# Three float32r passes over exactly split operands in place of seven- and twenty-product float32 schemes, in a scan and SwiGLU kernel

## The chip, the core and the metric

The kernel runs on one core of one Trainium2 chip. The metric is the device time of one execution in microseconds. The kernel before takes 394.63 us (median of 3 runs, 394.61 to 395.21).

## What is computed

A selective-state scan (Mamba-2) over 4 sequences, 8 heads, 768 positions, 32 channels a head and 16 states, followed by a feed-forward network over the resulting 3072 tokens of 256 channels. All arrays of the scan are float32; the three weight matrices come in as float64 in memory. Cut to what matters:

```python
for c in range(nc):                                   # chunks of 32 positions
    cum = np.cumsum(log_a[:, :, sl], axis=-1)
    L = np.exp(cum[:, :, :, None] - cum[:, :, None, :]) * causal
    y[:, :, sl] = einsum(CB * L, xc) + einsum(Cc, state) * np.exp(cum)[..., None]
    state = decay_full * state + sum_j(Bc * xc * decay_from_j)
x = y.transpose(0, 2, 1, 3).reshape(3072, 256)
xn = x / np.sqrt(np.mean(x * x, -1, keepdims=True) + 1e-06) * rms_g
g = xn @ w_gate                                       # 256 x 1536
out = (g / (1 + np.exp(-g)) * (xn @ w_val)) @ w_out   # 1536 x 256
```

## The kernel before

**Tiling.** The 3072 tokens are 6 blocks of 512. A block is two pairs of scan chunks of 128 tokens (12 pairs in all). The channels of a token lie on the partitions, so `xn` is two tiles of 128 x 512; the 1536 features are 12 tiles of 128, taken as 6 pairs `j` of feature tiles.

**Weights.** They are fetched as 18 pieces of 4 KB a partition (`fetch`, line 164/167, into 6 rotating places), and decoded from float64 words to float32: the power of two on ScalarE (`power`, three steps at line 197), the mantissa on VectorE (`mantissa`, lines 216 and 219), their product on VectorE (`weight`, line 225).

**Scan.** For each pair, decays are spread by DMA from memory (`spread`), subtracted, exponentiated and masked (`ex`), B and C are transposed on TensorE (`turn`, line 529), products formed (`products_of_block`, line 579) and multiplied by the decays (line 612), states carried on (`states`, lines 658 and 668), and the outputs formed (`outputs`, lines 644 and 716). `squares`, `norm_sums`, `norm_roots` and `norm_apply` (line 827) make `xn`. This is done for block b + 1 while block b's network runs.

**Gate and value products.** Blocks 1 to 5, and half of block 0's feature tiles, use a scheme of seven products for a 2 x 2 split (`product_gv`, line 931; its operands' sums are made by `combine_w` and `combine_x`). Each product k for a pair j is two matmuls (gate and value) of 128 x 128 weights by 256 columns. Partial sums are copied out by ScalarE (`taken_gv`, line 937) and added by VectorE (`total_gv`, line 943); then activation (line 197) and the hidden product (`hide_gv`, line 956, on VectorE or GpSimd). The rest of block 0 uses whole matmuls of 512 columns (`products_gv`, line 845) or, for the first two tiles, products of the values before normalization (line 855).

**Down products.** Block 0: 48 whole matmuls of 256 columns (`project`, line 963). Blocks 1 to 5: a scheme of twenty products for a 4 x 3 by 3 x 2 split (`product_o`, line 1052), each four matmuls of 128 columns; sums of hidden tiles (`sum_h`, line 1026) and of weights (line 1008) feed it, and `total_o` adds the products up in 26 steps (lines 1079 and 1083).

**Order.** A list of steps written out by hand gives the order in which every engine's instructions are issued; `idle` steps and `*2` marks put matmuls on constants into gaps. All matmuls are float32, but for bfloat16 matmuls on masks and constants (`idle`, line 317, and the fillers at line 88 among them). One matmul instruction in float32 appears in the trace as two weight loads and two matmul records.

Of the kernel before, what the change touches and what calls it, by code (L numbers as in the profile page):

```python
# [9 lines left out]
FP32 = mybir.dt.float32  # L10
I32 = mybir.dt.int32
# [5 lines left out]
AX = mybir.AxisListType  # L17


@with_exitstack  # L20
def kernel(
# [12 lines left out]

# [17 lines left out]
    NAR = BH * NC // 2  # L72

    const = ctx.enter_context(tc.tile_pool(name="const", bufs=1))
    raw = ctx.enter_context(tc.tile_pool(name="raw", bufs=3))
    ssd = ctx.enter_context(tc.tile_pool(name="ssd", bufs=2))
    cvt = ctx.enter_context(tc.tile_pool(name="cvt", bufs=2))
    nrm = ctx.enter_context(tc.tile_pool(name="nrm", bufs=2))
    ffn = ctx.enter_context(tc.tile_pool(name="ffn", bufs=2))
# [3 lines left out]

    fillers = []

    def filled(t, flat):
        for k in range(fillers.pop() if fillers else 0):
            nc.tensor.matmul(out=flat, lhsT=warm[:, 0:P], rhs=warm[:, 0:flat.shape[1]], start=True,
                             stop=True)
        return t  # L90

    def bank(name, shape):
        t = mm.tile(list(shape), FP32, tag="one", bufs=2, name=name)
        letters = "abc"[0:len(shape) - 1]
        flat = t.rearrange("p %s -> p (%s)" % (" ".join(letters), " ".join(letters)))
        return filled(t, flat[:, 0:min(256, flat.shape[1])])

    def pair_of_banks(name, slot):
        t = (mm if slot == 2 else pairs[slot].pool).tile([P, 2, 512], FP32, tag="pair%d" % slot,
                                                         name=name)  # L100
        return filled(t, t[:, 0, 0:256])


    pairs, later, sides = {}, {}, ("left", "right")
    for slot in (1, 0):
        pairs[slot] = ctx.enter_context(ExitStack())
        pairs[slot].pool = pairs[slot].enter_context(
            tc.tile_pool(name="first%d" % slot, bufs=1, side=sides[slot],
                         space=bass.MemoryType.PSUM))
# [4 lines left out]
    def load(p, queues=(nc.sync, nc.sync)):  # L114
        br = raw.tile([P, 2, NH, N], FP32, tag="br", name="br")
        cr = raw.tile([P, 2, NH, N], FP32, tag="cr", name="cr")
        st.setdefault(p, {}).update(B=br, C=cr)
        for i, queue in enumerate(queues):
            load_chunk(p, i, queue)
# [7 lines left out]
    def load_x(p, queue=nc.sync):  # L127
        b, c0 = divmod(2 * p, NC)
        st.setdefault(p, {})["x"] = raw.tile([P, 2, NH, D], FP32, tag="xr", name="xr")
        for i in range(2):  # L130
            sl = slice((c0 + i) * P, (c0 + i + 1) * P)
            queue.dma_start(out=st[p]["x"][:, i], in_=x[b, :, sl, :].rearrange("h s n -> s h n"))


    wgv = const.tile([P, 2, 2, DF], FP32, name="wgv")
    wg, wv = wgv[:, 0], wgv[:, 1]
    wo = const.tile([P, NF, DM], FP32, name="wo")
# [15 lines left out]
    def fetch(*ks):  # L153
        for k in ks:
# [7 lines left out]
            r = raw.tile([P, shape[0], 2 * shape[1]], I32, tag="wr", name="wr", bufs=6)  # L162
# [9 lines left out]

# [20 lines left out]
    def power(k):  # L199
        words16, (lo, hi), dst, shape = fetched[k]  # L200
        n = shape[1] * shape[2]
        e = cvt.tile([P, n], FP32, tag="e", name="e", bufs=4)
# [5 lines left out]
                             alpha=2.0 ** -20)  # L208
        activation(out=b16, in_=g, func=AF.Prelu, scale=-2.0 ** 27, bias=kinks[:, 2:3],
                             alpha=2.0 ** -20)  # L210
        parts[k, "e"] = b16.bitcast(BF16)

    def mantissa(k):
        words16, (lo, hi), dst, shape = fetched[k]
        m = cvt.tile(shape, I32, tag="m", name="m")
# [5 lines left out]

    def weight(k):
        words16, (lo, hi), dst, shape = fetched[k]
        e, f = parts.pop((k, "e")), parts.pop((k, "f"))
        nc.vector.scalar_tensor_tensor(out=dst, in0=f, scalar=2.0 ** -20, in1=e,  # L225
                                       op0=ALU.mult, op1=ALU.mult)

    a_sb = ffn.tile([NAR, 2 * P], FP32, tag="ob", name="a_sb", bufs=1)
# [3 lines left out]
    ones = const.tile([P, P], FP32, name="ones")  # L232
    upto = const.tile([P, P], FP32, name="upto")
    never = const.tile([P, P], FP32, name="never")
    after = const.tile([P, P], FP32, name="after")
    chunk_ones = const.tile([P, 2, P], FP32, name="chunk_ones")
# [7 lines left out]
    ident16 = const.tile([P, P], BF16, name="ident16")  # L244
    whole16 = const.tile([P, P], BF16, name="whole16")
# [4 lines left out]
    la = const.tile([P, NC, BH], FP32, name="la")  # L250
    laf = la.rearrange("p c h -> p (c h)")
    NG = 2 * NC * NB + 4
    early = nrm.tile([P, NC * BH + 2 * NG * NH], FP32, tag="xn", name="early", bufs=1)
    la0 = early[:, 0:NC * BH].rearrange("p (c h) -> p c h", c=NC)
    full, fsel = [early[:, NC * BH + k * NG * NH:][:, 0:NG * NH].rearrange(
        "p (g h) -> p g h", h=NH) for k in range(2)]
    la4 = [const.tile([P, 4, 4, NH], FP32, name="la4%d" % k) for k in range(2)]
    mids = const.tile([P, 2, P], FP32, name="mids")
    mid = mids[:, 0]
    first_four = slice(0, 4), slice(0, NH)  # L260

    def loaded_a():
        nc.sync.dma_start(out=a_sb, in_=a.rearrange("b h (q k) -> (b h q) k", k=2 * P))
# [50 lines left out]
    def idle(n):  # L314
        ps["idle"] = ps.get("idle") or bank("idle", (P, 256))
        for k in range(n):
            nc.tensor.matmul(out=ps["idle"], lhsT=warm[:, 0:P], rhs=warm, start=True, stop=True)

    def turn_a():
        ps["aT"] = aT = bank("aT", (P, 2, NAR))  # L320
        for k in range(2):
            nc.tensor.transpose(out=aT[:, k], in_=a_sb[:, k * P:(k + 1) * P],
                                identity=ident[0:NAR, 0:NAR])

    def clipped():
        nc.vector.tensor_scalar(
            out=la0.rearrange("p (q k) r -> p k r q", k=2),
            in0=ps.pop("aT").rearrange("p k (r q) -> p k r q", q=NC // 2), scalar1=1e-6,
            scalar2=1.0, op0=ALU.max, op1=ALU.min)

    def logs_again(g, n):
# [3 lines left out]
            in_=la0[:, c:c + n, b * NH:(b + 1) * NH].unsqueeze(2).to_broadcast([P, n, 4, NH]),  # L335
            func=AF.Ln)

    def minus_mid():
# [26 lines left out]
        "log": lambda: activation(out=la, in_=la0, func=AF.Ln), "mids": minus_mid,  # L365
# [7 lines left out]
    rows, ps = {}, {}  # L373

    def sums_of_logs(k):
        ps["r", k] = r_ps = bank("r_ps", (P, 2, P))
# [4 lines left out]
    def three_parts(k):  # L381
        r_ps = ps.pop(("r", k))
        first = nrm.tile([P, 2, P], BF16, tag="first", name="first", bufs=1)
        nc.vector.tensor_copy(out=first, in_=r_ps)
        rest = nrm.tile([P, 2, P], FP32, tag="rest", name="rest", bufs=1)
        nc.vector.scalar_tensor_tensor(out=rest, in0=first, scalar=later_part, in1=r_ps,
                                       op0=ALU.mult, op1=ALU.add)
        second = nrm.tile([P, 2, P], BF16, tag="second", name="second", bufs=1)
# [4 lines left out]

# [4 lines left out]
    def other_sums():  # L398
        ps["d"] = d_ps = bank("d_ps", (P, 2, NC, BH))
# [8 lines left out]
    def other_decays():  # L408
        activation(out=d_sb, in_=ps.pop("d"), func=AF.Exp)

# [3 lines left out]
    def chunk_sums():  # L414
        ps["c"] = full_ps = bank("full_ps", (P, NG * NH))
# [8 lines left out]
    def chunk_decays():  # L424
        activation(out=full.rearrange("p g h -> p (g h)"), in_=ps.pop("c"), func=AF.Exp)
        nc.gpsimd.tensor_tensor(out=fsel, in0=full,
                                in1=hmask.unsqueeze(1).to_broadcast([P, NG, NH]), op=ALU.mult)

    def chunk_column():
        nc.vector.reduce_sum(out=fcol, in_=fsel, axis=AX.X)  # L430


    Ls = {}

    def pair_tile(g):
        p = g // 2
        if p not in Ls and p < 4:
            Ls[p] = ssd.tile([P, 2, NH, P if p < 2 else HC], FP32, tag="L", name="L", bufs=2)
        elif p not in Ls:
            Ls["of", p // 2] = L = ssd.tile([P, 4, NH, HC], FP32, tag="L", name="L", bufs=2)  # L440
            for k in range(2):
                Ls[p - p % 2 + k] = L[:, 2 * k:2 * k + 2]
        return Ls[p][:, g % 2]
# [7 lines left out]
    def sums(p, half, e):  # L451
# [6 lines left out]
        for k, h in enumerate(heads):  # L458
            for i, r in enumerate(rows_of):
                for u in parts:  # L460
                    nc.tensor.matmul(out=e[u, i, k * n:(k + 1) * n],
                                     lhsT=sel[r, h:h + 1].to_broadcast([32, n]),
# [10 lines left out]
    def decay(p, half, e):  # L473
        pair_tile(2 * p)
        L = Ls[p][:, :, 4 * half:4 * half + 4] if p < 2 else Ls[p]
# [9 lines left out]
    def spread(g):  # L485
        b, c = divmod(g, NC)
        o = (c * BH + b * NH) * HC
        for u, r in enumerate(halves):
            nc.sync.dma_start(out=pair_tile(g)[r].rearrange("p h m -> p (h m)"),
                              in_=rowv[u, o:o + NH * HC].partition_broadcast(HC))  # L490

    def subtract(g, engine=nc.vector):
        b, c = divmod(g, NC)
        L = pair_tile(g)
# [4 lines left out]
    def exponential(g):  # L499
        L = pair_tile(g)  # L500
        activation(out=L, in_=L, func=AF.Exp)
        causal(L)

    def decays(g):
        subtract(g)
        exponential(g)

    def scale(p):
# [3 lines left out]
        for name, src, d in (("Cd", "C", to_i), ("Bd", "B", from_j))[0 if p < 2 else 1:]:  # L512
            s[name] = ssd.tile([P, 2, NH, N], FP32, tag=name, name=name)
            nc.vector.tensor_tensor(
                out=s[name], in0=s[src],
                in1=d[:, c0:c0 + 2, hs].unsqueeze(3).to_broadcast([P, 2, NH, N]), op=ALU.mult)

    def transposed(p):
        s = st[p]
        if "T" not in s:  # L520
            s["T"] = ssd.tile([P, 2, 4, P], FP32, tag="T", name="T")
        return s["T"]

    def turn(p):
        s = st[p]
        ps["t", p] = tp = bank("tp", (P, 2, 2, P))
        for k, src in enumerate((s["B"], s["C"])):
            for i in range(2):
                nc.tensor.transpose(out=tp[:, k, i], in_=src[:, i].rearrange("p h n -> p (h n)"),
                                    identity=ident)  # L530

    def turned(p, copy):
        copy(out=transposed(p)[:, :, 0], in_=ps["t", p][:, 0])

    def turned_of(p, scaled, t):
        scaled(transposed(p)[:, :, 1 + t], ps["t", p][:, 1], tmask[:, t:t + 1])

    def turned_of_both(p):
        shape = [P, 2, 2, P]
        nc.vector.tensor_tensor(  # L540
            out=transposed(p)[:, :, 1:3], in0=ps["t", p][:, 1].unsqueeze(2).to_broadcast(shape),
# [917 lines left out]
```

## Time and profile before

| what | value |
|---|---|
| median of the runs | 394.63 us |
| the profiled execution: its span from first to last instruction | 395.6 us |
| matmul records | 3833 |
| VectorE, ScalarE, GpSimd busy | 287.7, 233.6, 160.8 us |
| TensorE clock granted, mean | 0.999 of full |
| memory read, written | 22.64, 3.74 MB |

The profiled execution has no time of its own beside its span; the span is 1.0 us above the median. Spans of instructions include the latency of the engine, so what an instruction occupies is read from the distance of starts. "PE" is TensorE's matmuls and "PEld" its weight loads, "DVE" VectorE, "ACT" ScalarE, "POOL" GpSimd, "SP" the queue that issues most DMAs. "L931" is line 931 of the kernel before.

### The profile page before, as it was taken

The numbers are of one execution on the slowest core, as the hardware profiler recorded it, in microseconds if no ns is written. First come the engines' busy times: TensorE is split into PE (matmuls) and PEld (weight loads), VectorE is DVE, ScalarE is ACT, GpSimd is POOL, SyncE is SP. The second block draws the span as 40 slices with busy tenths as digits, with TensorE's granted clock in tenths as the row PEclk, the third lists the DMA queues.
The fourth block names the chain that finished last, engine by engine and source line by source line (L and its number), as shares of the span: only waits on it lengthen the run. The fifth ranks groups of instructions, "written<-read, shape, count | busy, mean of one in ns | idle before, by whom it ended". The sixth has DMA issues, their size and how long they took to land.

```text
span 395.6 us, 9626 instructions
## 1 busy us (share of the span) xinstructions
PE 387.5 (98%) x3833; PEld 331.9 (84%) x3833; DVE 287.7 (73%) x588; ACT 233.6 (59%) x483; POOL 160.8 (41%) x178
## 2 busy tenths in 40 slices
PE   8998999999999999999999999999999999999996
PEld 5674488878888899888889888899888899988995
DVE  6998999988657968484897765676754487465574
ACT  3988987968689393446661543676345750455410
POOL 2243253774638467102573610465402064211271
PEclk9999999999999999999999999999999999999999
DMA  8889985486002428201414002001100000100001
GB/s 125 220 161 245 203 164 155 142 170 133 0 1 68 56 83 137 83 2 30 107 35 83 13 2 68 2 15 36 42 1 3 0 8 27 55 0 2 2 2 53
DMA packets 92533, 27.01 MB, mean 68 GB/s; under 512 B 77416, under 2 KB 86344, under 8 KB 92488
## 3 DMA queue, kind: packets, MB, share of 16 engines
q1 hardware_dynamic: 90408, 26.26, 29.7%
q8 instruction: 30, 0.49, 0.5%
q10 hardware_dynamic: 2080, 0.13, 0.4%
q14 instruction: 15, 0.12, 0.1%
HBM read 22.64 MB, written 3.74 MB: 67 GB/s over the span
## 4 chain that ended last, share of the span: by engine, by line
PE 77%; DVE 10%; ACT 3%; issue 3%; DMA 3%; SPq 3%; DVEq 0%; ACTq 0%
PE gate L931 26%; PE o L1052 21%; PE val L931 19%; PE o L963 3%; PE y L716 2%; SPq L125 2%; DVE m L219 2%; DMA sq<-roots 1%; DMA br<-in_B_dram 1%; PE g L579 1%; DVE m L216 1%; ACT L L197 1%; DVE wgv L225 1%; DVE S L668 1%; DVE c L943 1%
## 5 line engine op out<-in xcount | busy, mean ns | idle before, releaser
L943 DVE TENSOR_TENSOR c<-val,p 128x512 f32<-128x512 f32 x99 | 67.5, 687 | 40.2 <-PE val L931 27.7
L937 ACT COPY p<-gate 128x512 f32<-128x512 f32 x99 | 56.8, 582 | 60.7 <-PE gate L931 56.1
L956 POOL TENSOR_TENSOR hid<-c 128x256 f32<-128x256 f32 x40 | 32.9, 830 | 84.8 <-ACT c L197 82.5
L931 PE MATMUL gate<-tx,wgv 128*128 128x256 f32 x264 | 65.8, 383 | 0.0
L197 ACT ACTIVATE c<-c 128x256 f32<-128x256 f32 x99 | 39.3, 415 | 29.2 <-DVE c L943 28.8
L931 PEld LDWEIGHTS gate<-tx,wgv 128*128 128x128 f32 x264 | 48.9, 190 | 7.9 <-issue 0.7
L956 DVE TENSOR_TENSOR hid<-c 128x256 f32<-128x256 f32 x59 | 30.1, 519 | 17.8 <-ACT c L197 17.8
L1083 DVE TENSOR_TENSOR ob<-ob,o 128x128 f32<-128x128 f32 (+1 forms) x90 | 24.5, 299 | 20.9 <-PE o L1052 18.0
L482 POOL TENSOR_SCALAR_AFFINE_SELECT L<-L 64x512 f32<-64x512 f32 (+1 forms) x36 | 29.3, 813 | 19.9 <-ACT L L197 13.1
L1052 PE MATMUL o<-two,hid 128*128 128x128 f32 x280 | 36.3, 276 | 0.1
L1052 PEld LDWEIGHTS o<-two,hid 128*128 128x128 f32 x280 | 34.4, 192 | 1.1 <-issue 0.2
L931 PE MATMUL val<-tx,sw 128*128 128x256 f32 x132 | 33.9, 382 | 0.0
L931 PE MATMUL val<-xn,sw 128*128 128x256 f32 x132 | 33.7, 380 | 0.0
L931 PE MATMUL val<-xn,wgv 128*128 128x256 f32 x132 | 33.4, 381 | 0.2 <-DVE c L943 0.2
L931 PE MATMUL gate<-tx,sw 128*128 128x256 f32 x132 | 33.4, 382 | 0.0
L931 PE MATMUL gate<-xn,wgv 128*128 128x256 f32 x132 | 33.3, 381 | 0.0
L931 PEld LDWEIGHTS val<-xn,wgv 128*128 128x128 f32 x132 | 24.8, 190 | 4.0 <-PE gate L931 0.6
L931 PEld LDWEIGHTS val<-tx,sw 128*128 128x128 f32 x132 | 24.9, 190 | 3.8 <-DVE c L943 0.3
L931 PEld LDWEIGHTS gate<-xn,wgv 128*128 128x128 f32 x132 | 24.5, 190 | 3.8 <-DVE xn L827 0.4
L197 ACT ACTIVATE u<-gate 128x256 f32<-128x256 f32 (+1 forms) x37 | 14.8, 403 | 21.8 <-PE gate L931 19.4
L931 PEld LDWEIGHTS gate<-tx,sw 128*128 128x128 f32 x132 | 24.5, 190 | 3.4 <-issue 0.2
L931 PEld LDWEIGHTS val<-xn,sw 128*128 128x128 f32 x132 | 24.4, 190 | 3.3 <-issue 0.2
(196 smaller groups left out, 741.3 us busy)
## 6 DMA issues: line engine op xcount, KB each, us to landing
L<-rowd SPq DMA_DIRECT2D x32, 128.0 KB, 3.2
xr<-in_x_dram SPq DMA_DIRECT2D x24, 128.0 KB, 3.6
wr<-in_moe_w_out_dram SPq DMA_DIRECT2D x6, 512.0 KB, 3.8
out_dram<-ob SPq DMA_DIRECT2D x24, 128.0 KB, 2.0
wr<-in_moe_w_gate_dram SPq DMA_DIRECT2D x5, 512.0 KB, 4.0
wr<-in_moe_w_val_dram SPq DMA_DIRECT2D x5, 512.0 KB, 6.9
br<-in_B_dram SPq DMA_DIRECT2D x23, 64.0 KB, 3.5
cr<-in_C_dram SPq DMA_DIRECT2D x23, 64.0 KB, 2.7
```

Of the source, the lines that this page charges most:

```text
L125: queue.dma_start(out=st[p][name][:, i], in_=src[b, :, sl, :].rearrange("h s n -> s h n"))
L197: nc.scalar.activation(**operands)
L219: nc.vector.scalar_tensor_tensor(out=f, in0=lo.bitcast(U32), scalar=2.0 ** -32, in1=m, op0=ALU.mult, op1=ALU.add)
L482: nc.gpsimd.affine_select(out=L[r], in_=L[r], pattern=[[0, L.shape[1]], [1, HC]], compare_op=ALU.is_ge, fill=0.0, base=0, channel_multipli ...
L716: nc.tensor.matmul(out=y[2 * k + u][rows, (2 * n + i) * HC:(2 * n + i + 1) * HC], start=(k, u, rows.start) not in opened, stop=True, skip_ ...
L931: nc.tensor.matmul(out=dst[:, half[w]], lhsT=lhsT, rhs=rhs, start=(k in (1, 2, 5) and w == 0), stop=True, skip_group_check=True)
L937: nc.scalar.copy(out=t, in_=Xs[j])
L943: nc.vector.tensor_tensor(out=t, in0=Zs[j], in1=a, op=ALU.add)
L956: engine.tensor_tensor(out=hid[:, 2 * j + c // 10 - 1, c % 10 - 1], in0=u, in1=src[:, half[1]], op=ALU.mult)
L963: nc.tensor.matmul(out=o, lhsT=hid[:, f, k // 2, (k % 2) * P:(k % 2 + 1) * P], rhs=wo[:, f], start=opens, stop=(f == NF - 1), skip_group_c ...
L1052: nc.tensor.matmul(out=Os[blk, b][:, place * P:(place + 1) * P], lhsT=hidden_or_sum(u)[:, g], rhs=rhs, start=(blk, b) not in opened, stop= ...
L1083: nc.vector.tensor_tensor(out=o, in0=o, in1=src, op=ALU.add if what[0] == "+" else ALU.subtract)
```

## The change

1. **Gate and value products of blocks 1 to 5.** Every operand is split into a high part (float32r, the value times 1 - 2^-13, rounded on writing) and what is left. Three passes of float32r matmuls replace the seven-product scheme: high by high, scaled rest by rest (`X`, both into one bank), then ScalarE multiplies that bank in place by 1 + 2^-12 (`sc`), and a pass of mixed operands is added (`M`). All matmuls have 512 columns. The scheme's sums, the copies out of the banks and the additions go.
2. **Down products of blocks 1 to 5.** The same three passes, 256 columns each, over feature tiles 0 to 5 and 6 to 11 (`OX`, `os`, `OM`). The hidden tiles are split after the hidden product: high (ScalarE or VectorE), low (VectorE or GpSimd), mixed (VectorE). The twenty-product scheme with its sums and its 26 additions goes; an output bank is copied out once.
3. **Block 0** has ten of its twelve feature tiles as whole float32 matmuls of 512 columns; the first two and the down products stay in form.
4. **Weights** get a high, a low and a mixed part each, into the place of the raw words; each of the 18 pieces has a place of its own.
5. **Places.** All tiles on the chip come from shared rings of equal places (`Ring`, `Place`), with counted uses; the banks for products are three pairs and two single ones.
6. **Order.** The list of steps is new from the first to the last. Activation tables are loaded 32 times, before 26.

The diff, cut to its core (the new list of steps is left out, but for a stretch of it):

```diff
+class Ring:
+    def take(self, uses, what):
+        return Place(self, self.free.pop(0), uses, what)
...
-    wgv = const.tile([P, 2, 2, DF], FP32, name="wgv")
+    wgv = const.tile([P, 2, 2, DF], F32R, name="wgv")
...
-            r = raw.tile([P, shape[0], 2 * shape[1]], I32, tag="wr", name="wr", bufs=6)
+            whole = const.tile([P, 1024], I32, tag="wr%d" % k, bufs=1, name="wr")
...
+    def weight_high(k, scaled):
+        scaled(fetched[k][2], view(ws[k], fetched[k][3]), BELOW)
+    def weight_low(k, engine=nc.vector):
+        engine.tensor_tensor(out=low_parts[k], in0=view(ws[k], shape), in1=dst, op=ALU.subtract)
+    def weight_mixed(k):
+        first, scalar, second = (dst, -DOWN, low) if pieces[k][0] == "o" else (low, -UP, dst)
+        nc.vector.scalar_tensor_tensor(out=mixed, in0=first, scalar=scalar, in1=second,
+                                       op0=ALU.mult, op1=ALU.add)
...
-    def combine_w(j, k, engine=nc.vector):
-    def combine_x(blk, k, engine=nc.vector):
-    def product_gv(blk, k, j):
-    def taken_gv(blk, k, j):
-    def total_gv(blk, c, j):
-    def sum_h(blk, n, engine=nc.vector):
-    def total_o(blk, n):
...
+    def x_high(blk, t, scaled):
+        scaled(view(b, [P, TB], F32R), xns[blk][1][:, t], BELOW)
+    def x_mixed(blk, t):
+        nc.vector.scalar_tensor_tensor(out=view(b, [P, TB], F32R), in0=view(hb, [P, TB]),
+                                       scalar=-1.0 - DOWN, in1=xns[blk][1][:, t], op0=ALU.mult,
+                                       op1=ALU.add)
+    def x_scaled(blk, t):
+        nc.vector.scalar_tensor_tensor(out=view(b, [P, TB], F32R), in0=view(mb, [P, TB]),
+                                       scalar=UP, in1=view(hb, [P, TB]), op0=ALU.mult,
+                                       op1=ALU.add)
...
+    def gv_product(o, blk, f, m, t, x_part, w_part, start):
+        nc.tensor.matmul(out=o, lhsT=weights_of(m, t, f)[w_part], rhs=view(b, [P, TB], F32R),
+                         start=start, stop=True, skip_group_check=True)
+    def gv_whole(blk, f, m):
+        for t in range(2):
+            nc.tensor.matmul(out=o, lhsT=view(ws[k], fetched[k][3])[:, t, f % 2 * P:][:, 0:P],
+                             rhs=xn[:, t], start=(t == 0), stop=(t == 1))
+    def gv_split(blk, f, m):
+        o = gv_bank(blk, f, m, True)
+        for part in range(2):
+            for t in range(2):
+                gv_product(o, blk, f, m, t, part, part, part == 0 and t == 0)
+    def gv_scaled(blk, f, m):
+        activation(out=o, in_=o, func=AF.Copy, scale=1.0 + DOWN)
+    def gv_mixed(blk, f, m):
+        for t in range(2):
+            gv_product(o, blk, f, m, t, 2, 2, False)
...
+    def hid_high(blk, f, scaled):
+        scaled(view(b, [P, TB], F32R), view(hx[blk, f], [P, TB]), BELOW)
+    def hid_low(blk, f, engine=nc.vector):
+        engine.tensor_tensor(out=view(b, [P, TB], F32R), in0=view(hx[blk, f], [P, TB]),
+                             in1=view(hh[blk, f], [P, TB]), op=ALU.subtract)
+    def hid_mixed(blk, f):
+        nc.vector.scalar_tensor_tensor(out=view(b, [P, TB], F32R), in0=view(hl[blk, f], [P, TB]),
+                                       scalar=-UP, in1=view(b, [P, TB]), op0=ALU.mult,
+                                       op1=ALU.add)
+    def product_o(blk, b, v, w):
+        for j in range(2):
+            tk = slice((2 * b + j) * P, (2 * b + j + 1) * P)
+            nc.tensor.matmul(out=o_bank(b)[:, j * DM:(j + 1) * DM], lhsT=v[:, tk], rhs=w,
+                             start=(blk, b) not in begun, stop=True, skip_group_check=True)
+    def o_scaled(blk, b, k):
+        activation(out=o, in_=o, func=AF.Copy, scale=1.0 + DOWN if k % 2 == 0 else
+                   1.0 / (1.0 + DOWN))
...
     order = """
+        p:scale.5 i:pow.15 b:hid.0.11 i:wt.17 i:wHv.10 p:Tt.5.1 b:exps.1 b:OF.0.8.1 i:wM.1 b:X.1.1.0
+        b:OF.0.4.1 b:X.1.1.1 b:sc.1.1.0 b:hid.0.10 i:wt.15 i:wLp.13 i:wM.0 b:X.1.0.0 b:sc.1.0.0
+        p:x.5 p:Tt.5.0 b:M.1.1.0 b:OF.0.7.1 b:sc.1.1.1 i:wM.7 b:X.1.0.1 i:wL.6 i:wM.3 i:wM.4
```

In the list, `b:X.1.1.0` is block 1, feature tile 1, gate (0) or value (1); `b:OF.0.8.1` is block 0's down products of feature tile 8 for the token tiles of half 1; `i:wM.1` is the mixed part of weight piece 1; `p:` are steps of a scan pair.

More of the change, by code (lines that the diff above doesn't have):

```diff
@@ L10 @@
 FP32 = mybir.dt.float32
+F32R = mybir.dt.float32r
 I32 = mybir.dt.int32
@@ L89, in filled, with bank @@
                              stop=True)
[L90 to L109, printed above, removed]
+    def bank(shape, uses, what):
+        b = one.take(uses, what)
+        v = view(b, shape)
+        if fillers:
+            filled(view(b, [P, 256]))
+        return b, v
     st = {}
     def load(p, queues=(nc.sync, nc.sync)):
-        br = raw.tile([P, 2, NH, N], FP32, tag="br", name="br")
-        cr = raw.tile([P, 2, NH, N], FP32, tag="cr", name="cr")
-        st.setdefault(p, {}).update(B=br, C=cr)
+        s = st.setdefault(p, {})
+        s["bc"] = b = h.take(2, "bc")
+        s["B"], s["C"] = [view(b, [P, 2, 2, NH, N])[:, k] for k in range(2)]
         for i, queue in enumerate(queues):
@@ L424, in chunk_decays, with pair_tile @@
     def chunk_decays():
-        activation(out=full.rearrange("p g h -> p (g h)"), in_=ps.pop("c"), func=AF.Exp)
+        b, full_ps = ps.pop("c")
+        full, fsel = ps["full"], ps["fsel"]
+        activation(out=full.rearrange("p g h -> p (g h)"), in_=full_ps, func=AF.Exp)
         nc.gpsimd.tensor_tensor(out=fsel, in0=full,
                                 in1=hmask.unsqueeze(1).to_broadcast([P, NG, NH]), op=ALU.mult)
+        b.used()
+        ps["early"].used()
     def chunk_column():
[L430 to L443, printed above, removed]
+        nc.vector.reduce_sum(out=fcol, in_=ps["fsel"], axis=AX.X)
+        ps["early"].used()
+    Ls, Lp = {}, {}
+    def pair_tile(p):
+        if p not in Ls:
+            if p < 2:
+                Ls[p] = lead.tile([P, 2, NH, P], FP32, name="L%d" % p)
+            else:
+                Lp[p] = q4.take(2, "L")
+                Ls[p] = view(Lp[p], [P, 2, NH, HC])
+        return Ls[p]
     def mask(e):
@@ new lines, with gv_mode, uses_of_x, take @@
+    O4 = {(0, 1), (0, 7), (0, 4), (0, 10), (0, 0), (0, 3), (0, 9), (0, 6), (0, 2), (0, 5), (0, 8), (0, 11)}
+    def gv_mode(blk, f):
+        return 0 if blk == 0 and f < 2 else 4 if (blk, f) in GV4 else 3
+    def uses_of_x(blk):
+        return 4 * (3 in modes(blk)) + 2 * modes(blk).count(4)
+    us, hx, hh, hl = {}, {}, {}, {}
+    def take(key):
+        held[key] = banks = picks.pop(0)
+        assert not any(v in (banks, (banks, 0), (banks, 1)) for k, v in held.items() if k != key)
+        return banks2[banks]
@@ L1253 @@
     }
     order = """
-        0:warm 0:a 0:set 0:bc.0 0:ident 0:bc.1 0:bc2.1.1 0:ones 0:zeros 0:ident16 0:whole 0:kinks
-        0:idle.7 0:after 0:never 0:fetch.2 0:whole16 0:mean 0:part 0:head 0:part2 0:sel 0:after2
-        0:mask.0.0/0 0:upto 0:mid 0:upto2 0:eps 0:aT 0:la0 0:hmask 0:x.0 0:mask.0.1/1 0:mids
-        0:log4.0.4 0:log4.4.2 0:mask.1.1/2 0:fetch.0 1:exps 0:tmask 0:r.0 0:parts.0 0:log 0:d 0:c*2
-        0:dx 0:turn.0 0:gcol 0:sums.0.1 0:scale.0 0:sums.1.1 0:cx 0:scale.1 0:sums.0.0 0:Tb.0 0:T.0
@@ L1415 @@
-        5:w.23 5:put.1 5:O.10.0 5:O.10.1 5:w.21 5:w.24 5:w.25 5:put.2
+        i:ones i:upto i:a i:ident i:fetch.1 i:whole i:mid i:ident16 i:hmask i:bc.0 i:tmask i:head
+        b:exps.2 i:part i:aT i:zeros i:never i:la0 i:mids i:log4.0.4 i:kinks i:r.0 i:whole16
+        i:log4.4.2 i:part2 i:upto2 i:mask.1.1/2 i:log i:after i:eps i:after2 i:sel i:middles i:d
+        i:warm i:mask.0.0/0 i:mask.0.1/1 i:bc.1 i:mean i:parts.0 i:pow.1 i:sums.0.1 p:turn.0 i:dx
+        i:man.1 i:Tb.0 i:sums.1.1 i:exp.0.1 i:log4.6.2 i:exp.1.1 i:bc2.1.1 i:c*2 p:T.0 i:fetch.2
@@ new lines @@
+        i:sums.0.0 p:x.0 p:scale.0 i:cx i:g.0.1/1 p:turn.1 i:exp.0.0 i:L.0.1 p:Tt.1.0 i:r.1
+        i:mask.1.0/1 i:g.0.0/0 i:fetch.0 p:T.1 p:Tt.1.1 i:pow.2 p:scale.1 i:idle.7 i:cc i:last.0
+        i:sums.1.0 i:g.1.0/2 i:parts.1 i:Tl.0 i:last.1 i:L.0.0 i:A.0 i:g.1.1/0 i:Tl.1 i:exp.1.0
+        p:S.0 i:pow.0 p:x.1 i:gcol i:L.1.0 i:fetch.6 i:fetch.4 i:row.1 i:set i:y.0/1 i:sq.0 i:L.1.1
+        i:fetch.3 i:rowe.1 p:bc.2 i:A.1 i:fetch.5 p:S.1 i:y.1/2 i:rowout.1 i:yt.0 i:ydone.0 i:sq.1
+        i:row.0 i:yt.1 i:sums.3/1 i:exp.3 i:wt.1 i:ydone.1 i:fetch.12 i:man.2 i:rowe.0 i:pow.4
```

1274 lines of the change are left out of this document (659 added, 615 removed), and 15 rows, old and new, of tables (COMBOS, FACTORS, SUMS, TOTALS).

## The prediction

> **What bounds the kernel now.** I read the page first: busy time by engine, then the chain that ended last.
>
> ```profile
> PE 387.5 (98%) x3833; PEld 331.9 (84%) x3833; DVE 287.7 (73%) x588; ACT 233.6 (59%) x483; POOL 160.8 (41%) x178
> PE 77%; DVE 10%; ACT 3%; issue 3%; DMA 3%; SPq 3%; DVEq 0%; ACTq 0%
> ```
>
> TensorE is on 77% of the chain, but its 98% overstates it: a record's duration includes the fill of the pipeline. So I cut the span where one token block's gate and value products end and the next ones' begin (each cut is the start of the group of records with which the count of line 931 completes a block). Columns: stretch, its length, busy us (and instructions) of PE, PEld, DVE, ACT and POOL, clock, DMA share, GB/s.
>
> ```profile
> 0.00:77.40 77.40, 73.70 (x869) 50.46 (x870) 71.73 (x160) 63.61 (x116) 29.73 (x44) 1.00 0.79 176
> 254.10:311.00 56.90, 56.90 (x589) 51.32 (x588) 34.99 (x72) 31.61 (x71) 22.07 (x23) 1.00 0.06 17
> 311.00:363.20 52.20, 52.20 (x326) 47.66 (x326) 32.49 (x65) 23.92 (x56) 16.14 (x16) 1.00 0.05 17
> ```
>
> There are two regimes. In the opening (77.4 us: float64 weights decoded, first chunks of the scan, block 0) VectorE works 71.7 us, 93% of the time, and paces it. From there on TensorE never rests (56.9 of 56.9, 52.2 of 52.2) and VectorE is busy for 62%. A gain must come from TensorE's time in the second regime, and any added VectorE work ahead of it counts against the gain.
>
> What one product really occupies is read from the chain, where merged pieces carry start, length and count:
>
> ```profile
> 85.26 1.73 PE val L931 x8
> 91.30 1.73 PE o L963 x8
> 323.39 11.36 PE o L1052 x100
> ```
>
> A float32 matmul stands as two records. One of 256 columns takes 1.73/8 = 0.216 us a record, one of 128 columns 11.36/100 = 0.114. The totals by line (PE and PEld busy):
>
> ```profile
> 0.00:395.60 395.60, 209.09 (x924) 172.00 (x924) 1.00 0.31 68
> 0.00:395.60 395.60, 95.70 (x800) 93.49 (x800) 1.00 0.31 68
> ```
>
> The first row is line 931, gate and value: 924 records = 462 matmuls, that is 7 products x 2 matrices x 6 pairs of feature tiles x 5.5 blocks. The second is line 1052, the down products of blocks 1 to 5: 800 records = 5 x 80 matmuls.
>
> **The missing price.** No row shows a float32r matmul. Its neighbours (start, length, count):
>
> ```profile
> 7.40 0.39 PE L88 MATMUL full_ps<-warm 128*128 128x256 bf16 x2 [0.15 <-DVE rest L386]
> 7.62 0.82 PE L418 MATMUL full_ps<-la,chunk_ones 128*128 128x192 f32 x4
> 46.03 3.60 PE L845 MATMUL gate<-xn,wgv 128*128 128x512 f32 x8
> 49.56 0.49 PE L716 MATMUL y<-T,S 32*64 32x64 f32 x32
> ```
>
> Two bf16 matmuls of 256 columns start 0.22 us before the next kind: 0.110 each, half of a float32 record, so a record streams its columns twice and a float32 matmul four times. Eight records of 512 columns take 49.56 - 46.03 = 3.53 us, 0.882 a matmul. So 512 columns of float32r cost between 0.216 (once through) and 0.882 (four times), 256 columns between 0.110 and 0.432. I take once: an operand rounded beforehand has no second half to be fetched, which makes bf16 its nearest row; with the pitch of 0.114 for 256 columns, since its weight load is a four-byte one as in line 1052. The page "FP8 and Floating Point Precision" of the Trainium skill, section "TensorE Precision Notes", counts four passes for true float32 and describes a reduced float32 that is truncated as it is read; by it, too, one pass, and the same sum.
>
> **Part by part, blocks 1 to 5.**
> - Gate and value: out go 5 x 84 = 420 matmuls of 2 records, 840 x 0.216 = 181.4 us. In come per block 12 feature tiles x 2 matrices x 3 passes x 2 halves of the contraction = 144 matmuls of 512 columns, 720 in all, x 0.216 = 155.5. Net -25.9.
> - Down: out 800 x 0.114 = 91.2. In 12 x 4 token tiles x 3 = 144 matmuls of 256 columns per block, 720 x 0.114 = 82.1. Net -9.1.
>
> Gains are that small because seven products for eight and twenty for twenty-four had already been saved; three passes for four only improves on this.
>
> **Block 0.** Out 42 matmuls of line 931 (84 x 0.216 = 18.1) and 16 of line 845 (16 x 0.882 = 14.1); in 40 whole float32 matmuls of 512 columns (35.3). Net +3.1. Its down products stay 48 float32 matmuls, the early products stay 16. The scan's matmuls keep their counts, and so cost 0.
>
> **The opening.** VectorE's durations (mean ns is the number behind the comma):
>
> ```profile
> L943 DVE TENSOR_TENSOR c<-val,p 128x512 f32<-128x512 f32 x99 | 67.5, 687 | 40.2 <-PE val L931 27.7 <-ACT p L937 8.6 <-POOL hid L956 3.5
> L1026 DVE TENSOR_TENSOR hid<-hid 128x512 f32<-128x512 f32 x19 | 15.8, 833 | 0.8 <-POOL hid L956 0.4
> L219 DVE SCALAR_TENSOR_TENSOR m<-wr,m 128x512 f32<-128x512 uint32 x18 | 14.9, 828 | 0.6
> L216 DVE TENSOR_SCALAR m<-wr 128x512 int32<-128x512 int32 x18 | 8.8, 489 | 0.0
> L225 DVE SCALAR_TENSOR_TENSOR wgv<-m,e 128x512 f32<-128x512 f32 x12 | 8.1, 685 | 0.1
> L827 DVE SCALAR_TENSOR_TENSOR xn<-yt,gcol,sq 128x512 f32<-128x512 f32 x10 | 7.1, 752 | 0.5 <-DMA sq<-roots 0.5
> L668 DVE SCALAR_TENSOR_TENSOR S<-S,fcol,A 128x64 f32<-128x64 f32 x36 | 13.0, 362 | 1.0
> L878 DVE TENSOR_TENSOR hid<-u,gate 128x512 f32<-128x512 f32 x4 | 2.7, 681 | 0.0
> ```
>
> Block 1's first accumulated pass needs the mixed weights of tile 1 (`weight_mixed`). I compared the instructions ahead of it on VectorE with the 160 of the first 77.4 us before. More now: three mantissa pairs (3 x 1.317), three weights (3 x 0.685), five hidden products less three half ones (about 2.2), nine high parts at line 216's 0.489 (4.4), three mixed and six x parts at 0.752 (6.8), two low parts and one subtraction at 0.833 (2.5): 21.9. Fewer: seven states (2.5), seven line 943 sums (4.8), and combinations and additions of some 4.5: 11.8. Net +10.1 on 71.7; at the same 93% the opening ends at about 88 us, +10.9. TensorE is not idle in it: half of block 0's down products now stand ahead of block 1 (24 matmuls of 0.432, against 8 before: +6.9), with the +3.1 above. So the opening costs 10.9 - 10.0 = +0.9. Writing float32r may cost more or less than these float32 rows: 18 such writes, each off by at most the 0.34 between lines 216 and 219, bound this at 6 either way; I take 0, the same shapes.
>
> The queue on SP also changes: 18 places for raw weights instead of 6, so that no fetch waits for a place, and the B and C loads behind it are freed. The chain held them long here:
>
> ```profile
> 21.25 3.38 SPq L125
> 26.56 4.58 DMA br<-in_B_dram
> 20.00:40.00 20.00, 18.30 (x190) 11.85 (x179) 18.80 (x33) 16.95 (x28) 9.16 (x8) 1.00 0.93 202
> ```
>
> In these 20 us VectorE was busy for 18.8: what the freed queue can give is 1.2, and I count 0, with VectorE next.
>
> **The added work beside TensorE.** ScalarE gets 120 scalings of a bank between passes two and three and 30 of the down banks.
>
> ```profile
> L937 ACT COPY p<-gate 128x512 f32<-128x512 f32 x99 | 56.8, 582 | 60.7 <-PE gate L931 56.1 <-DVE c L943 2.6 <-DVE wgv L225 1.0
> L191 ACT ACT_TABLE_LOAD x13 | 16.7, 1283 | 1.0 <-PEq L1443 0.8
> L197 ACT ACTIVATE u<-gate 128x512 f32<-128x512 f32 x4 | 2.4, 592 | 2.2 <-DVE hid L878 2.2
> ```
>
> At line 937's 0.582 that is 87.3 us; with 70 activations of 512 (0.592 by four such records, about 41), some 46 high parts and copies (about 29) and six more table loads (7.7), against 99 copies, 99 + 37 activations and 40 output copies that go (about 124), ScalarE stands near 275 of 234 before. VectorE comes to about the same: 194 go, some 181 come. Per block of the second regime that is about 40 us on each, under some 52 of TensorE. I count 0: a bank's round (0.86 of products, 0.58 scaling, 0.43, 0.59 activation: 2.5 us) fits twice into the 5.2 that the four banks' products take. GpSimd only loses work. With that cover gone, each of the 120 third passes would wait 0.58 and more, and so would all behind it on TensorE, which takes its matmuls in order.
>
> **The end.** The last feature tile has to pass activation, product, high, low and mixed part (0.59 + 0.68 + 0.49 + 0.83 + 0.75 = 3.3 us) before its last down pass. The first passes of the half's other five tiles stand ahead of it on TensorE (20 x 0.114 = 2.3), So up to 3 us may show, of which the end before has as much:
>
> ```profile
> 380.00:395.60 15.60, 12.06 (x104) 11.52 (x102) 8.31 (x23) 0.96 (x4) 5.76 (x5) 0.98 0.11 35
> ```
>
> TensorE rests there for 3.5 us of the 15.6, and I count 0.
>
> **The sum.** 395.6 - 25.9 - 9.1 + 3.1 + 0.9 = 364.6 us of span. The shown median of 394.6 is 1.0 below the profiled span, so **364 us**.
>
> **Rivals.**
> 1. ScalarE becomes the pace. For it: 275 us of 365 busy, unevenly, table loads of 1.28 and the decoding in the way of scalings. Against: 12 us of slack per block. If a third pass waits 0.1 to 0.25 us, 120 of them take 12 to 30: 376 to 394. Chance 0.13, nearly all still faster.
> 2. **Slower: a column of float32r is not one pass.** It strikes 1440 matmuls that I priced at 155.5 + 82.1 = 237.6. The forecast's gain of 31 is gone at 1.13 times the price, 0.244 us for 512 columns; at twice, it is 364 + 238 = 602. For it: line 845's float32 needs four, and no trace shows this format. Against: bf16's one. Chance 0.10.
> 3. **Slower: the weight load is exposed.** Line 1052's loads:
>
> ```profile
> L1052 PEld LDWEIGHTS o<-two,hid x280: 186/192/193, 132.8 to 391.2; 128*128 128x128 f32 x140
> ```
>
> If the loads of 0.192 set the pitch of the 256-column passes, 720 x (0.192 - 0.114) = 56 is added: 420. If every one stood bare, 1440 x 0.192 = 276: 640. It decides from 31/1440 = 0.022 us exposed per matmul. Against: a hundred records, each with such a load, started every 0.114. Chance 0.05. The page "TensorE: Matmul & The Clock Gate" of the Trainium skill, section "Part 3: Packing small matmuls", says that a load overlaps a running matmul only if it is for other rows of the array; this trace does not agree, since these loads use all 128 rows and 0.192 fits into 0.114 only by overlap.
> 4. Gain and added waits cancel: within 0.2%, about what a measurement here can tell. 0.02.
>
> **How the numbers follow.** Forecast 0.70, rivals 0.13, 0.10, 0.05, 0.02. Rival 1 leaves 0.01 beyond 394; so faster 0.82, same 0.02, slower 0.16. The range runs from 352 (float32r writes 6 cheaper, and 6 of the waits behind the opening's 7% idle gone) to rival 1's 394: left out are rivals 2 and 3 and a little below.
>
> **What would show it.** Float32r records of 512 columns pitched at 0.216 and of 256 at 0.114, one a matmul; the first float32r product at 85 to 92 us; after it TensorE without rest, and hardly any idle put down to the scaling; table loads 32. I am wrong if the pitch is above 0.244, if TensorE sits waiting for ScalarE for over 10 us, or if VectorE delays block 1 beyond 100 us.

## The result, and the profile after

The changed kernel takes **457.5 us** (median of 4 runs, 456.8 to 460.4); the kernel before took 394.9 beside it (median of 4, 394.6 to 395.3). The ratio is 1.159, interval 1.156 to 1.163: slower by 16%, where 364 us were forecast.

The page's busy times:

```profile
PE 399.7 (88%) x3597; PEld 301.7 (66%) x3597; DVE 283.4 (62%) x502; ACT 281.2 (62%) x490; POOL 109.9 (24%) x107
```

ScalarE and VectorE are as busy as the prediction counted (275 us each). TensorE, with 236 records fewer than before, stands at 88%: no engine is full. The same cuts as before, by stage (length, busy us of PE, PEld, DVE, ACT and POOL, clock, DMA share, GB/s):

```profile
0.00:98.00 98.00, 85.78 (x813) 50.97 (x813) 86.06 (x166) 74.10 (x124) 29.56 (x35) 1.00 0.65 148
98.00:140.00 42.00, 37.95 (x306) 28.78 (x310) 26.10 (x49) 20.64 (x34) 13.81 (x13) 0.93 0.38 59
140.00:430.00 290.00, 259.13 (x2372) 207.28 (x2372) 160.07 (x272) 180.38 (x321) 63.83 (x58) 0.99 0.14 33
```

The opening lasts until 98 instead of 88. After it TensorE rests 31 us of the 290 in the third row, where before it rested for none; VectorE works 55% of that time and ScalarE 62%. So this is waiting, not load. The view of waits says who waits for whom (engine, tile and line, released by; us, times, longest); line 231 is every activation, 1138 the hidden product, 1100 a gate or value product, 1176 a down product:

```profile
ACT pair L231 <- PE pair L1100: 73.0, 47, 8.4
DVE hx L1138 <- PE pair L1100: 69.2, 25, 7.6
PEld pair L1100 <- ACT pair L231: 21.3, 28, 2.1
DVE hx L1138 <- ACT pair L231: 20.1, 8, 4.3
PEld pair L1100 <- DVE hx L1138: 15.8, 16, 2.8
PE pair L1100 <- DVE hx L1138: 14.8, 12, 3.8
PE pair L1100 <- ACT pair L231: 13.4, 18, 1.7
ACT pair L231 <- DVE hx L1138: 9.7, 7, 2.3
```

Read against the code, the fourth and the last row are the odd ones. An activation that writes `pair` is the scaling. A hidden product needs the sum after the third pass, which TensorE adds *after* the scaling; data can never make it wait for a scaling. Nor can a scaling need a hidden product, which reads a finished bank. The third group of experiments takes these two rows up.

### The profile page after: what moved, and what is told of

Same layout as the page of the kernel before. It is cut to its first block, busy times and chain, and to the rows that moved or that the text cites. A ratio compares the mean times of both kernels' runs of the same rounds, so it can differ in the third digit from the quotient of the medians.

```text
span 455.1 us, 8950 instructions
## 1 busy us (share of the span) xinstructions
PE 399.7 (88%) x3597; PEld 301.7 (66%) x3597; DVE 283.4 (62%) x502; ACT 281.2 (62%) x490; POOL 109.9 (24%) x107
## 5 line engine op out<-in xcount | busy, mean ns | idle before, releaser
L231 ACT ACTIVATE pair<-pair 128x512 f32<-128x512 f32 x150 | 84.7, 582 | 103.4 <-PE pair L1100 73.0
L1138 DVE TENSOR_TENSOR hx<-hx,pair 128x512 f32<-128x512 f32 x70 | 47.7, 685 | 110.6 <-PE pair L1100 69.2
L1100 PE MATMUL pair<-xh,wgv 128*128 128x512 f32 x240 | 82.2, 424 | 18.9 <-DVE hx L1138 12.1
L1100 PE MATMUL pair<-xm,wp 128*128 128x512 f32 x240 | 78.5, 419 | 16.2 <-ACT pair L231 8.9
L1100 PE MATMUL pair<-xl,wp 128*128 128x512 f32 x240 | 76.0, 398 | 0.0
L231 ACT ACTIVATE hx<-pair 128x512 f32<-128x512 f32 x70 | 41.0, 595 | 33.0 <-PE pair L1100 24.0
L1100 PEld LDWEIGHTS pair<-xl,wp 128*128 128x128 f32 x240 | 46.0, 191 | 11.0
L1157 DVE SCALAR_TENSOR_TENSOR hh<-hl,hh 128x512 fp32r<-128x512 f32 x60 | 43.7, 750 | 14.1 <-PE pair L1176 13.9
L1176 PE MATMUL pair<-wo,hh 128*128 128x256 f32 x240 | 48.8, 285 | 3.3 <-ACT pair L231 2.2
L1176 PE MATMUL pair<-wp,hl 128*128 128x256 f32 x240 | 47.8, 280 | 0.0
```

The lines of the kernel that those rows point to most:

```text
L231: nc.scalar.activation(**operands)
L1100: nc.tensor.matmul(out=o, lhsT=weights_of(m, t, f)[w_part], rhs=view(b, [P, TB], F32R), start=start, stop=True, skip_group_check=True)
L1138: nc.vector.tensor_tensor(out=v, in0=v, in1=gv_bank(blk, f, 1), op=ALU.mult)
L1157: nc.vector.scalar_tensor_tensor(out=view(b, [P, TB], F32R), in0=view(hl[blk, f], [P, TB]), scalar=-UP, in1=view(b, [P, TB]), op0=ALU.mult ...
L1176: nc.tensor.matmul(out=o_bank(b)[:, j * DM:(j + 1) * DM], lhsT=v[:, tk], rhs=w, start=(blk, b) not in begun, stop=True, skip_group_check=True)
```

## The experiments

**First: is it the added work?** Three parts of it were taken away, one at a time, from the changed kernel. The 150 scalings:

```diff
     def gv_scaled(blk, f, m):
-        activation(out=o, in_=o, func=AF.Copy, scale=1.0 + DOWN)
+        pass
     def o_scaled(blk, b, k):
-        activation(out=o, in_=o, func=AF.Copy, scale=...)
+        pass
```

> Left out: the 150 scalings of product banks between the passes (120 gate and value, 30 down), so the output lacks a factor of 1 + 2^-12 on two of the three passes; all else as after. Theory A (the scaling puts a second round trip through ScalarE into every bank's use, and TensorE, in order, stands behind it): the 24 us of gaps before third gate/value passes and the 13 before down passes go, and half of the 29 before first passes, since banks come free earlier: 457 falls to about 400 (395 to 412). Theory B (the gaps come from VectorE's load and from the release of banks by the hidden product): only the gaps that are put down to the scaling itself go: 430 to 440. Theory C (a float32r column costs more than one pass): 455, nothing moves.

Measured: 425.9 us (425.4 to 426.9). So 31.6 us hang on the scalings, and the other 31 above the kernel before on something else; the time lies between the ranges of theories A and B and decides for neither. In the waits, the hidden products take the place of the scalings ahead of the gate and value products:

```profile
PEld pair L1100 <- DVE hx L1137: 18.4, 20, 1.9
PE pair L1100 <- DVE hx L1137: 16.5, 16, 3.8
```

The 60 mixed parts of the hidden tiles, and then the table loads (Relu in place of Silu, so that 31 loads go):

```diff
     def hid_mixed(blk, f):
-        nc.vector.scalar_tensor_tensor(out=..., in0=..., scalar=-UP, in1=..., ...)
+        pass
```

> Left out: the 60 mixed parts of hidden tiles on VectorE (0.75 us each, 44 us in all); the third down pass reads the high part as it stands. The scalings stay. Theory A: under 8 us less than 457, since VectorE is 62% busy. Theory B (VectorE's load): 15 to 35 us less. Theory C: no change.

> Changed: the activation of the gate is a ramp (Relu), which needs no table of its own, in place of Silu, so that 31 of the 32 table loads (1.28 us each, 41 us of ScalarE) go; everything else stays. Theory A: each load sits now and then ahead of a scaling: 5 to 20 us less than 457. A rival within A, that ScalarE's total work is the pace: 30 to 40 less. Theories B and C: under 5.

Measured, one run each: 455.9 and 449.7 us. The two pages, without the mixed parts and without the loads:

```profile
PE 399.7 (88%) x3597; PEld 301.3 (66%) x3597; DVE 239.7 (53%) x442; ACT 281.6 (62%) x490; POOL 106.7 (23%) x107
```

```profile
PE 397.2 (89%) x3597; PEld 299.5 (67%) x3597; DVE 283.8 (63%) x502; ACT 241.7 (54%) x459; POOL 109.6 (24%) x107
```

Taking 44 us of busy time from VectorE gave under 2, which the scatter of the changed kernel's own runs covers; taking 40 from ScalarE gave 8. The load of either engine, taken alone, is not what TensorE mainly waits for.

**Second: is it the scheme of passes, or the list?** A plain split in two parts (high by high, low by high, high by low; no scaled or mixed parts) leaves out the scaling and the product of the two low parts, with the same matmuls:

> Changed: three passes of plain high and low parts (high x high, low x high, high x low; low x low is left out), all added into one bank with no scaling between, so that the mixed and scaled parts go too: 150 instructions of ScalarE, some 60 + 18 + 10 of VectorE less; TensorE's matmuls, the order of the steps and the places as after. Theory A: as without the scalings and some less, 385 to 400, and, if the new list of steps were free of gaps, 357 of TensorE's work plus some 20. Theory B: 400 to 415, as VectorE loses 65 us. Theory C: 440 or more.

Measured: 412.2 us (410.6 to 413.5), with this page:

```profile
PE 383.3 (94%) x3597; PEld 298.1 (73%) x3597; DVE 218.4 (53%) x410; ACT 200.1 (49%) x338; POOL 102.9 (25%) x107
```

With 65 us less VectorE and 81 us less ScalarE work than the changed kernel it is still 4.5% slower than before. That is inside theory B's range, but B's cause, VectorE's load, had brought under 2 us when 44 us of it were taken away. Two changes of its list follow. Each third pass is put right behind the first two:

```diff
-  b:X.1.1.0 b:OF.0.4.1 b:X.1.1.1 b:sc.1.1.0 ... b:M.1.1.0
+  b:X.1.1.0 b:M.1.1.0 b:OF.0.4.1 b:X.1.1.1 b:M.1.1.1 ...
```

> The two-part split of e4 with one more change: in the list of steps each third gate/value pass stands directly behind the first two of its bank (nothing lies between them that it needs), so that a bank's six matmuls run in one piece; activation, hidden product and all else stay where they stood. Theory A2 (what is left of the loss is banks held open while TensorE is busy elsewhere, so that the next first pass waits for the release): e4's 17.6 us of gaps ahead of first passes halve and e4's 412 falls to 398 to 405. Theory D (the new list of steps itself is uneven on the in-order engines, and the opening is paced by VectorE): within 5 us of 412.

Measured: 407.3 us (407.2 to 407.9), 4.9 less: above theory A2's range and at the edge of theory D's. Then each activation and hidden product is put right behind its third pass, so that a bank comes free as early as its data allow:

> As e5, and the activation and the hidden product of each feature tile stand directly behind the third pass that they need, on ScalarE's and VectorE's queues, in place of some steps later. Theory A2: banks come free as early as the two engines allow: 392 to 400. Theory D: 405 to 412, and engines that wait for third passes may hold up what stands behind them, up to 420.

Measured: 432.0 us (431.2 to 432.5), 25 worse and outside both ranges. I took this for the cost of engines that stand at their next instruction in order. With the theory of the next experiment it reads otherwise, though no run separated the two: a hidden product directly behind its own bank's last pass stands ahead of the *other* bank's next products.

**Third: the tile.** All three attempts had kept one thing: two banks lie in one tile. (A tile is a buffer as the kernel declares it; a bank is here 512 float32 columns of it, which take one sum of products.)

```diff
-    banks2 = [mm.tile([P, 2, 512], FP32, name="pair%d" % k) for k in range(3)]
+    banks2 = [[mm.tile([P, 512], FP32, name="pair%d" % (2 * k + m)) for m in range(2)]
+              for k in range(3)]
```

The program sets a wait between two accesses of a tile whenever one of them writes, and here it does so whichever of the two banks they touch. In the program as built, the 120 scalings of gate and value banks carry 128 waits: 43 name the bank's own products, 82 a step on the other bank of the tile (18 a third pass, 12 a first, 18 a hidden product, 19 a scaling, 15 an activation), 3 a step of the scan. The timeline of the changed kernel shows the first of them (start, us, engine, line, what, and in brackets idle time and releaser):

```profile
98.10 1.19 PE L1100 MATMUL pair<-xh,wgv 128*128 128x512 f32 x2 [3.77 <-DVE hx L1138]
99.09 1.06 PE L1100 MATMUL pair<-xl,wp 128*128 128x512 f32 x2
...
101.30 1.42 PE L1100 MATMUL pair<-xh,wgv 128*128 128x512 f32 x2
102.51 1.06 PE L1100 MATMUL pair<-xl,wp 128*128 128x512 f32 x2
...
103.60 0.58 ACT L231 ACTIVATE pair<-pair 128x512 f32<-128x512 f32 x1 [8.40 <-PE pair L1100]
```

The gate bank has its four products at 100.15 (99.09 + 1.06). ScalarE has been idle for 8.40 us, and `sc` of that bank is its next instruction. It starts at 103.60, just after 102.51 + 1.06 = 103.57, the end of the four products of the *value* bank. The first row has the same fault: the gate bank waits for the hidden product that reads the value bank of an earlier feature tile.

Six tiles of one bank, the same list, and 22 instructions that use both banks at once cut in two:

> The changed kernel with one edit: each of the six product banks is a tile of its own, where the changed kernel holds two banks in one tile (gate and value of a feature tile, or the two halves of the output). Same list of steps, same arithmetic; 20 instructions that read both banks of a pair at once become two of half the size. Theory T (two banks in one tile are put in order with each other: a scaling, an activation or a product of one bank waits for the step before it in the list on the other bank): the waits that the changed kernel's view shows ahead of the gate, value and down products for scalings, activations and hidden products, 21.3 + 15.8 + 14.8 + 13.4 + 11.5 + 6.6 + 8.1 = 91.5 us, mostly go: all gone would be 457.5 - 91.5 = 366 us, a third left 396; I expect 370 to 396. Rival Q (the engines' own order and load make the waits, as I read the runs until now): 445 to 460.

Measured: **397.6 us** (397.2 to 398.3), ratio to before 1.005 (1.002 to 1.008), 1.6 us above the range that theory T gave and far from rival Q's. 60 of the 93 us between forecast and result hang on this one line. (Theory T's 91.5 us added the waits of weight loads and of products, which stand at the same time. Between the two pages TensorE's idle time falls from 55.4 to 15.1 us, its busy time from 399.7 to 381.1.) Its page, and its stages:

```profile
PE 381.1 (96%) x3597; PEld 298.4 (75%) x3597; DVE 287.7 (73%) x516; ACT 280.1 (71%) x498; POOL 108.5 (27%) x107
```

```profile
0.00:94.90 94.90, 86.09 (x814) 51.04 (x814) 84.14 (x169) 73.79 (x132) 26.53 (x33) 1.00 0.64 150
94.90:140.00 45.10, 43.07 (x478) 33.00 (x477) 37.47 (x66) 28.44 (x52) 18.51 (x18) 1.00 0.42 69
140.00:382.00 242.00, 241.69 (x2227) 204.42 (x2226) 158.17 (x272) 173.52 (x309) 61.93 (x57) 1.00 0.16 38
```

From 140 us on TensorE works 241.69 of 242.00 us, under the same ScalarE and VectorE work. Of the waits above, this is what is left ahead of the gate and value products:

```profile
PEld pair L1106 <- DVE hx L1144: 3.0, 4, 1.4
PE pair L1106 <- DVE hx L1144: 1.3, 2, 0.9
PEld pair L1106 <- ACT pair L232: 0.4, 2, 0.2
```

The two odd rows, of a hidden product that waits for a scaling and the reverse, are gone from the view. The scaling that started at 103.60 now follows its own bank at once (0.03 after 96.20 + 0.50):

```profile
96.20 0.50 PE L1106 MATMUL pair<-xl,wp 128*128 128x512 f32 x1 [0.30 <-DVE xl L1034]
96.53 1.03 PE L1182 MATMUL pair<-w,hx 128*128 128x256 f32 x4
96.73 0.58 ACT L232 ACTIVATE pair<-pair 128x512 f32<-128x512 f32 x1 [0.85 <-PE pair L1106]
```

The control has that kernel's code and instructions, but the six banks are again halves of three tiles:

> The control for it: the code of the run with six tiles, but the six banks are views of three tiles of two banks, as in the changed kernel. Both theories: 452 to 463 us, as the changed kernel (457.5): the 20 instructions that are now two of half the size cost under 4 us.

Measured: 458.6 us (457.2 to 460.1), ratio 1.162 (1.157 to 1.167). The two runs differ in the declaration of the tiles alone, so it is the tile, and not the cutting of instructions in two, that helped. Next, only the two output banks stay in one tile:

> Six tiles but for the two output banks, which stay in one tile. Theory T: the waits ahead of the down products for a scaling (8.1 us ahead of their weight loads in the changed kernel, 5.3 ahead of the products) come back, so 8 to 20 us above the run with six tiles. Rival Q: no more than 3 us from it.

Measured: 410.4 us (410.1 to 410.9), 12.7 above the six tiles; 11.8 us of waiting for a scaling stand ahead of the down products there:

```profile
PEld pair L1183 <- ACT pair L233: 7.1, 9, 1.1
PE pair L1183 <- ACT pair L233: 4.7, 8, 0.9
```

**Fourth: what does the scheme cost once the banks are free?**

> The kernel with the plain two-part split (412.2 us: no scaling, no mixed or scaled parts, the product of the two low parts left out), with each bank a tile of its own. Theory T: a scaling and the added VectorE and ScalarE work are hidden once a bank is free of its neighbour, so within 6 us of the run with six tiles and all the scalings. Rival R (the 32 us that leaving the scalings out brought were the scalings' own price): 25 to 45 us below that run.

> Six bank tiles as in the run of 397.6 us, and the 150 scalings of a bank left out (the products are then added up unscaled; everything else is as there). With banks in pairs, leaving them out brought 457.5 - 425.9 = 31.6 us. Theory T (a scaling cost time only because its bank's neighbour had to wait for it as well): no more than 6 us now, 391 to 398. Rival R (a scaling has a price of its own on the path): 20 us or more, 378 or less.

Measured: 389.5 us (388.9 to 390.0) for the two-part split, and 397.4 (397.0 to 397.5) for the scheme without its scalings. Against the runs with banks in pairs (the first row's is the control; the other two are the runs of the first and second group):

| | banks in pairs | a tile each | the pairing costs |
|---|---|---|---|
| three passes with scaling | 458.6 | 397.6 | 61.0 |
| without the 150 scalings | 425.9 | 397.4 | 28.5 |
| two-part split | 412.2 | 389.5 | 22.7 |

The scalings cost 32.7 us in the left column (31.6 against the changed kernel itself) and 0.2 in the middle one, which is within the scatter of the runs. What looked like their price in the first experiment was the price of their neighbours' waiting. The two-part split with a tile for each bank takes 1.5% less time than the kernel before: ratio 0.985 (0.982 to 0.989). It leaves out the product of the two low parts. It stands 8.2 us below the six tiles with the whole scheme, beyond the 6 that I had expected; its first block-1 product starts 2.1 us earlier (92.8 against 94.9), and where the rest comes from was not tested.

## Why the prediction was wrong

**The step that failed** is in the part on the added work beside TensorE: "I count 0: a bank's round (... 2.5 us) fits twice into the 5.2 that the four banks' products take." The arithmetic holds, but it takes four places, each free by itself. The kernel had "three pairs" of banks (part 5 of the change), each pair in one tile, and a pair moves in the order of the list: 61.0 us between the control and the run with six tiles. The same paragraph had named the price: "each of the 120 third passes would wait 0.58 and more, and so would all behind it". The cover was gone for a reason that stood in the code and not in any duration. With a tile for each bank the count of 0 is right for the scalings: 0.2 us for all of them. For the whole scheme's added work it is 8.2, the distance to the two-part split, of which 2.1 lie ahead of block 1.

**Rival 1** said ScalarE would be the pace, 376 to 394. The sign it gave, TensorE waiting for scalings, came (21.3 + 13.4 us in the waits), but not its cause: taking away 40 us of table loads gave 8 us.

**Rivals 2 and 3** are out. The price of a column came nearly as taken. From the chain of the run with six tiles (start, length, count):

```profile
209.20 3.23 PE pair L1106 x14
382.78 9.50 PE pair L1182 x80
```

3.23/14 = 0.231 us for 512 columns (taken: 0.216; break-even 0.244), 9.50/80 = 0.119 for 256 (taken: 0.114). So float32r takes one pass. The section "TensorE Precision Notes" of the Trainium skill's page "FP8 and Floating Point Precision" counts four for true float32 and gives no count for the reduced one; the prediction's one pass was read out of it, and these rows bear it out. The weight loads of 0.188 us stay hidden in a pitch of 0.119, so the rule in the section "Part 3: Packing small matmuls" of the Trainium skill's page "TensorE: Matmul & The Clock Gate", that a load overlaps a running matmul only for other rows of the array, does not hold for these full-array loads.

**What remains of the miss**, 397.6 against 364, is a sum of small terms, most of them missing from mine. The pitch: 720 x 0.015 + 720 x 0.005 = 14 us. The opening: the first product at 94.9 instead of 88, with 84.1 us of VectorE's work in it and not 81.8, at a share of 89% and not 93%: 7 us. VectorE is not its only pace: on the chain from 20 to 95 us the decoding of weights on ScalarE (`e`) stands for 12.6%, issuing the loads of B and C for 7.3% and waiting for raw weights to land for 5.3%. Waits between 94.9 and 140: 2 us. And the scan's matmuls, which I priced at 0 because their counts stay. Their busy time after the opening (behind the length of the stretch; first the products of B and C, then the outputs `y`), before at lines 579 and 716:

```profile
77.40:395.60 318.20, 4.82 (x256) 1.00 0.19 42
77.40:395.60 318.20, 10.17 (x752) 1.00 0.19 42
```

And with six tiles, at lines 707 and 868:

```profile
94.90:396.20 301.30, 5.18 (x256) 1.00 0.20 42
94.90:396.20 301.30, 13.59 (x752) 1.00 0.20 42
```

The same 256 and 752 records occupy 18.8 us where they occupied 15.0, 3.8 more: fewer of the outputs' records overlap, at the same length of each. I saw this in the trace alone and did not test why. The four terms make 27 of the 33.6 us. About what is left lies in the pitch again: by the distances of their starts in the trace, the 720 products of 512 columns stand 0.242 us apart over the whole run, and not the 0.231 of an unbroken row, which is 8 us.

**What held:** the bound by TensorE after the opening, but only once each bank had a tile (241.69 of 242.00 us); VectorE as the busiest of the other engines in the opening (86 of 98 us); and the load of the three other engines.

## What to carry to other kernels

When a change gives several buffers one tile, ask what the program will take for one thing: a pair of banks in one tile was a single place with two users, and cost 61 us of 459. In a view of waits, look first for a row that the data cannot explain (a product waiting for the scaling that comes before its own input); such a row is a false wait. Rotating products through banks, as the section "Matmuls" of the Trainium skill's page "Perfetto Trace Analysis" advises, was done here and did not overlap fully until each bank was a tile. Taking work away measures that work together with all who queue behind it: 150 scalings were worth 31.6 us or 0.2, depending on one line elsewhere.

## What the chip showed that I had not expected

A long wait at TensorE can cost more than its own length. When block 1's first product had waited for the neighbour's hidden product, the clock granted to TensorE fell to a half (third column from the end):

```profile
88.00:94.00 6.00, 6.00 (x21) 3.61 (x19) 5.72 (x9) 5.85 (x11) 2.77 (x2) 1.00 0.06 10
94.00:98.00 4.00, 0.34 (x2) 0.00 (x0) 4.00 (x5) 1.21 (x1) 3.08 (x3) 0.91 0.34 53
97.20:97.30 0.10, 0.00 (x0) 0.00 (x0) 0.10 (x2) 0.00 (x0) 0.00 (x0) 0.94 0.00 0
98.00:99.00 1.00, 0.90 (x2) 0.83 (x3) 1.00 (x3) 0.00 (x0) 0.00 (x0) 0.50 0.61 97
103.00:104.00 1.00, 1.00 (x4) 0.81 (x3) 1.00 (x3) 0.40 (x1) 1.00 (x1) 0.50 0.42 42
104.00:105.00 1.00, 1.00 (x5) 0.81 (x5) 0.31 (x1) 0.35 (x2) 1.00 (x1) 0.94 0.98 93
```

After 3.77 us of rest, two products of 512 columns took 0.99 us (98.10 to 99.09) instead of 0.46, and so it stayed for 6 us of steady work, from 98.10 to about 104.1: some 3 us lost beyond the wait. The section "Part 1: The HAM clock gate" of the Trainium skill's page "TensorE: Matmul & The Clock Gate" says that an idle window of about 3.4 us halves the clock. That is near what this trace shows, though here it came sooner: TensorE's last record before the rest ended at 94.34, and the clock fell just before 97.30, 2.9 us later. The section also gives about 3.4 us of sustained work as the time until the full clock returns; here it took 6.
